# A Nystrom attention and SiLU kernel: the first two batches' attention steps placed anew

## The chip, the cores and the metric

The kernel runs on one core of a Trainium2 chip. The metric is the device time of one execution in microseconds (us); lower is better. A core has five engines that run side by side, each with its own queue of instructions in program order: TensorE (PE, matrix products, whose weight loads the profile lists as PEld), VectorE (DVE), ScalarE (ACT), GpSimd (POOL) and SyncE (SP). POOL and SP issue the DMA transfers here. An instruction waits until what it reads is there and until the buffer that it writes is free; whatever stands behind it in its engine's queue waits with it.

## The reference, cut to what matters

Eight batches of eight heads go through Nystrom attention with 576 tokens, head width 64 and 32 landmarks; the result (4608 tokens of width 512) goes through a two-layer network with SiLU.

```python
q_lm = q.reshape(B, H, m, S // m, D).mean(axis=3)      # m = 32 landmarks of 18 tokens
k_lm = k.reshape(B, H, m, S // m, D).mean(axis=3)
A  = sm(q, k_lm)                                       # softmax of scaled scores
Bm = sm(q_lm, k_lm)
C  = sm(q_lm, k)
Z  = Bm.T / (norm1(Bm) * norm_inf(Bm) + 1e-06)
for _ in range(6):
    Z = 2 * Z - Z @ Bm @ Z
x = A @ Z @ C @ v          # then, over all heads side by side:
h = x @ w_in
out = (h * sigmoid(h)) @ w_out
```

## The kernel before, in words

The attention output x is never formed. For each batch the kernel computes W = C v (`w_mm`, `w_out`), multiplies it by Z (`x_out`, `z_mm`, `z_out`), and then by w_in, which gives a matrix called mb of 256 rows by 2048 columns (`m_unit` makes a quarter of it, `m_pair` two quarters). The first layer of the network is then A times mb (`l1_mm`, products that the profile calls hps), SiLU on ACT (`l1_act`, tile gT), and the second layer is gT times w_out (`l2_mm`, tile ops). These two layers of products fill PE for most of the time.

For each batch b the main loop has 16 steps s. The first eight handle the batch's first tokens (256 of 576 in batch 0, half in the others), the last eight the rest. In step s, `l1_mm(b, s)` makes four hps products, `act` runs SiLU on them, and `l2_mm(n)` issues the next n products of the output tiles that are queued (a tile of 128 tokens takes 16). How many is a table written by hand, `CNT` (lines 764 to 767). Between these, by hand as well, stand the steps of the next batch's attention: the order of instructions on each engine is exactly that of the program.

Batch 0 has nothing to hide behind. Its attention runs ahead of the loop, in lines 772 to 858. There q and k of the first four heads come in float32 over SP (line 122, tiles raw), the rest over POOL's queue (line 105), which casts on the way; DVE casts k (line 774), ACT casts q (line 775). `landmarks_pe` sums the 18 tokens of each landmark on PE (tile lmp), `landmarks_out` scales the sums on ACT (line 212), `transpose_qk` turns q and k on DVE (line 195), `lm_t` turns the landmarks on DVE (line 263), and `bd_expand` copies them into block diagonals (line 271). `b_scores` and `c_scores` are the scores of Bm and C; `b_norm`, `b_scale` and `f_out` prepare the Newton iteration, of which `ns_mm` is the products and `ns_step` the update. `c_exp` is exp(C), `c_transpose` and `c_out` turn it. A is made by `a_scores`, `a_max`, `a_shift`, `a_exp`, then a row sum, a reciprocal and a product on POOL (`a_sum`, `a_rec`, `a_mul`, together `a_norm`), and `a_transpose` and `a_out` bring it to the layout of the first layer (tile AT). Calls of `idle` issue products of zeros on PE, which keep it busy while it would wait.

Batch 1's attention runs inside batch 0's steps. There d is 2, so step s = d + r has r from 1 to 13; the steps from d + 1 on (lines 925 to 1050) carry it. Rest pieces of batch 0 run there too: w_in units 2 and 3 (lines 994 and 1003) and the second part of A (`a0.a_norm(1)`, `a0.a_norm(2)`, `a0.a_transpose(1)`), which `l1_mm(0, 8)` is the first to read.

PSUM buffers are few: pool psa has one (scores sa, products mp, atp, wp, zt), pool pso two (sa, mp, ctp, output tiles ops), pool psn one (lmp, bb). w_in comes in four parts and w_out in four (lines 140 and 145), all over POOL's queue, as do v (line 111) and the later q and k.

Of the kernel before, what the change touches and what calls it, by code (L numbers as in the profile page):

```python
# [40 lines left out]
def kernel(  # L41
# [56 lines left out]
    def load_qk(b, js=(1, 0, 3, 2)):  # L98
        if b not in nat_t:
            nat_t[b] = loadp.tile([128, 4, SEG * Dh], BF, tag="nat", name="nat")  # L100
        nat = nat_t[b]
        for j in js:
            src = (q, k)[j % 2]
            g = j // 2
            nc.gpsimd.dma_start(
                out=nat[:, j, :],
                in_=src[b, 4 * g:4 * g + 4].rearrange("h (l t) d -> (h l) (t d)", t=SEG))
# [21 lines left out]
    def idle(o, n, w=128):  # L129
        for _ in range(n):  # L130
            mm(o[:, 0:w], zero[:, 0:128], zero[:, 0:w], start=True, stop=True)
# [7 lines left out]
    def load_w_in(f):  # L139
        nc.gpsimd.dma_start(  # L140
            out=w_in_sb[:, :, 512 * f:512 * f + 512],
            in_=moe_w_in.rearrange("(j p) n -> p j n", p=128)[:, :, 512 * f:512 * f + 512])

    def load_w_out(j):
        nc.gpsimd.dma_start(
            out=w_out_sb[:, 4 * j:4 * j + 4, :],
            in_=moe_w_out[512 * j:512 * j + 512, :].rearrange("(c p) m -> p c m", p=128))

    load_w_in(0)
    load_qk(1, (1, 0))  # L150
    load_w_in(1)
    load_qk(1, (3, 2))
    load_w_in(2)
# [17 lines left out]

    xb = constp.tile([128, 2, 2 * L], BF, tag="xb", name="xb")
    nc.vector.memset(xb, 0.0)
    parity = constp.tile([128, 2], FP, tag="parity", name="parity")

    eC_t = []
# [59 lines left out]
    class Att:  # L236
# [76 lines left out]
        def b_norm(self):  # L313
            brec = attp.tile([128, 2], FP, tag="brec", name="brec")
            nc.vector.reciprocal(out=brec, in_=self.bsum)
            self.bm = attp.tile([128, 2, L], BF, tag="bm", name="bm")
            nc.vector.tensor_tensor(out=self.bm, in0=self.pb,
                                    in1=brec.unsqueeze(2).to_broadcast((128, 2, L)), op=OP.mult)
            self.bmt = attp.tile([128, 2, L], BF, tag="bmt", name="bmt")
            nc.vector.transpose(out=self.bmt, in_=self.bm)  # L320
            if not self.tiled:
                self.bdt = attp.tile([128, 2, 128], BF, tag="bdt", name="bdt", bufs=1)
                self.expand(self.bdt, self.bmt)
# [14 lines left out]

        def b_scale(self):
            cs = attp.tile([128, 2], FP, tag="cs", name="cs")  # L340
            nc.vector.tensor_reduce(out=cs, in_=self.bmt, op=OP.add, axis=AX.X)
            n1 = attp.tile([128, 2], FP, tag="n1", name="n1")
            nc.vector.tensor_reduce(out=n1, in_=cs.unsqueeze(2).to_broadcast((128, 2, L)),
                                    op=OP.max, axis=AX.X, apply_transpose=True)
            self.nrm = attp.tile([128, 2], FP, tag="nrm", name="nrm")
            w = self.fw = L if self.tiled else 128
            self.fx = nsp.tile([128, 2, w + L], BF, tag=f"fx{w}", name="fx", bufs=3)
            if self.tiled:
                nc.vector.tensor_scalar(out=n1, in0=n1, scalar1=1e-6, scalar2=-1.0, op0=OP.add,
                                        op1=OP.mult)  # L350
                nc.vector.reciprocal(out=self.nrm, in_=n1)
                nc.vector.tensor_tensor(
                    out=self.fx[:, :, w:w + L], in0=self.bm,
                    in1=self.nrm.unsqueeze(2).to_broadcast((128, 2, L)), op=OP.mult)
                return
            nc.vector.tensor_scalar(out=n1, in0=n1, scalar1=1e-6, scalar2=None, op0=OP.add)
            nc.vector.reciprocal(out=self.nrm, in_=n1)
            for g in range(2):
                nc.vector.tensor_scalar(out=self.fx[:, g, w:w + L], in0=self.bm[:, g, :],
                                        scalar1=self.nrm[:, g:g + 1], scalar2=None, op0=OP.mult)  # L360
# [254 lines left out]
        def a_sum(self, i):  # L615
            x, r = self.a_part(i)
            nc.vector.tensor_reduce(out=r, in_=x, op=OP.add, axis=AX.X)  # L617

        def a_rec(self, i, n=1):
            c, _, pr = self.a_dims(i)  # L620
            r = self.arec[0:pr, c:min(c + 2 * n, len(TCH)), :].rearrange("p c h -> p (c h)")
            nc.vector.reciprocal(out=r, in_=r)  # L622
# [118 lines left out]
    def l2_mm(n):  # L741

        st = l2_state
        while n > 0 and st["queue"]:
# [16 lines left out]
                nc.sync.dma_start(out=out[r0:r0 + 128, :], in_=ost)  # L761


    CNT = {0: [0, 0, 0, 0, 6, 4, 2, 2, 4, 2, 2, 2, 2, 2, 2, 2],
           1: [2, 2, 2, 2, 2, 6, 8, 8] + [4, 3] * 4,
           2: [5, 4, 12, 14, 3, 3, 3, 2, 4, 3, 3, 3, 4, 3, 3, 3]}
    REST = [5, 4, 12, 12, 3, 3, 2, 2, 4, 4, 4, 3, 4, 3, 4, 3]
# [1 line left out]

    ORD = (1, 0, 3, 2)  # L770
    wt = pso1("idle")
    idle(wt, 12, 512)
    lp = psn1("lmp")
    nc.vector.tensor_copy(out=nat_t[0][:, 1, :], in_=raw[1])
    nc.scalar.copy(out=nat_t[0][:, 0, :], in_=raw[0])  # L775
    transpose_qk(0, 1)
    landmarks_pe(0, lp, 0, 2)
    transpose_qk(0, 0)
    landmarks_out(0, lp, 0, 2)
    idle(wt, 2, 512)  # L780
    a = Att(0)
    a.lm_t(0)
    a.bd_expand(0, 1, nc.scalar.copy)
    landmarks_pe(0, lp, 3, 1)
    transpose_qk(0, 3)
    landmarks_out(0, lp, 3, 1)
    idle(wt, 2, 512)
    landmarks_pe(0, lp, 2, 1)
    transpose_qk(0, 2)
    landmarks_out(0, lp, 2, 1)  # L790
    idle(wt, 3, 512)
    a.lm_t(1)
    a.b_scores()
    a.bd_expand(1, 1, nc.gpsimd.tensor_copy)
    load_w_in(3)
    a.c_scores()
    a.b_max()
    a.b_exp()
    a.a_start()
    a.a_scores(0)  # L800
    idle(wt, 2, 512)
    a.c_max(0)
    a.c_exp(0)
    a.b_norm()
    a.f_mm()
    a.b_scale()
    a.f_out()
# [2 lines left out]
    a.c_out(0, nc.scalar.copy)  # L810
    a.ns_mm()
    a.c_max(1)
    idle(wt, 2, 512)
    a.ns_step()
    a.c_exp(1)
    a.ns_mm(whole=True)
# [1 line left out]
    a.ns_step(nc.scalar.copy)  # L818
    idle(wt, 1, 512)
    a.c_transpose(1)  # L820
    a.a_shift(0)
    a.a_exp(0)
    a.ns_mm()
    a.c_out(1, nc.scalar.copy)
    a.ns_step()
    a.a_sum(0)
    idle(wt, 1, 512)
    a.ns_mm()
    idle(wt, 2, 512)
    a.ns_step()  # L830
    a.w_scale()
    a.a_rec(0)
    a.a_mul(0)
    load_w_out(0)
    load_w_out(1)
    a.w_mm()
    a.ns_mm()
    a.w_out()
    table(AF.Silu)
    a.ns_step()  # L840
    idle(wt, 1, 512)
    a.ns_mm(last=True)
    a.x_out()
# [4 lines left out]
    a.z_mm(at[:, 1, :])  # L848
    a.z_out()
    lp = psn1("lmp")  # L850
    landmarks_pe(1, lp, 0, 2, (0, 6))

    def first_tokens():
        a.a_transpose(0, at[:, 0, :].bitcast(BF))
        a.a_out(nc.vector.tensor_copy)
        landmarks_pe(1, lp, 0, 2, (6, SEG))

    a.m_unit(0, nc.vector.tensor_copy, nc.scalar.copy, parts=2, between=first_tokens)

# [3 lines left out]
    for b in range(B):  # L863
# [14 lines left out]
        for s in range(NDC):  # L878
# [89 lines left out]
            elif s == d + 2:  # L968
# [20 lines left out]
                a.a_shift(2)  # L989
                a.a_exp(2)  # L990
                if b == 0:
                    a.b_scale()
                    l2_mm(4)
                    a0.m_unit(2, nc.vector.tensor_copy, nc.scalar.copy)
                    a.f_mm()
                    a.f_out()
                    l2_mm(n - 4)
                else:
                    l2_mm(n - 4 - min(n - 4, 6))
                table(AF.Silu)  # L1000
                l1(s)
                if b == 0:
                    a0.m_unit(3, nc.vector.tensor_copy, nc.vector.tensor_copy)
            elif b == 0:
                l1(s)
                r = s - d
                if r == 3:
                    act(s - 1)
                    a.ns_mm()
                    a.c_transpose(0)  # L1010
                    a.ns_step()
                    a.c_out(0, nc.scalar.copy)
                    a0.a_norm(1)
                    a0.a_norm(2)
                elif r == 4:
                    a.ns_mm()
                    a.c_transpose(1)
                    a.w_scale()
                    a.ns_step()
                    a.ns_mm()  # L1020
                    a.c_out(1)
                    a.a_norm(0)
                    a0.a_transpose(1)
                    a0.a_out(nc.scalar.copy)
                elif r == 5:
                    a.ns_step()
                    a.ns_mm()
                    a.a_norm(1)
                elif r == 6:
                    a.w_mm()  # L1030
                    a.ns_step()
                    a.ns_mm()
                    a.w_out()
                    a.ns_step()
                    a.a_norm(2)
                elif r == 7:
                    a.ns_mm(last=True)
                    a.x_out()
                    a.a_transpose(0)
                    a.a_out(nc.scalar.copy)  # L1040
                elif r == 8:
                    a.z_mm(psa1("zt"))
                    a.z_out()
                    l2_mm(cnt[s])
                    a.a_transpose(1)
                    a.a_out(nc.vector.tensor_copy)
                act(s)
                if r in (9, 11):
                    a.m_pair(r - 9)
                l2_mm(cnt[s] if r != 8 else 0)  # L1050
            elif s == d + 3:
                l1(s)
                act(s - 1)
# [114 lines left out]
```

## Time and profile before

| | us |
|---|---|
| median of 3 runs | 267.85 |
| the runs | 266.73, 267.85, 269.39 |
| the profiled execution, its own time | 265.98 |
| its span, first to last instruction | 264.0 |
| PE busy in the span | 254.0 |
| ACT, DVE, POOL busy | 174.3, 161.5, 117.0 |
| start of the first hps product of batch 0 | 23.05 |
| start of the hps products of steps 8 and 11 of batch 0 | 42.07, 47.70 |

The profile is one execution. Its times run from the start of the span. Rows of the timeline name the engine, the line in the kernel, the tile written and the tiles read, and in square brackets how long the engine was idle before and what released it. The chain of work that ended last is followed back from the last instruction, at each step to what released it. A line can be a helper's: line 77 is that of all products.

### The profile page before, as it was taken

How to read it: one execution, taken by the hardware profiler on the slowest of the kernel's cores; microseconds unless marked ns; L12 is line 12 of the kernel's file. 1: busy time of each engine (PE TensorE's matmuls, PEld its weight loads, DVE VectorE, ACT ScalarE, POOL GpSimd, SP SyncE). 2: the span in 40 equal slices, each digit the busy share in tenths (PEclk: the TensorE clock that was granted, in tenths of full speed). 3: DMA queues.
4: the chain of work that ended last, by engine and by line, in shares of the span. 5: the costliest groups of instructions: out<-in, count | busy, mean ns of one | idle time of the engine just before them, and what ended most of it. 6: DMA issues, size and time to landing. Idle time of an engine off the chain costs nothing.

```text
span 264.0 us, 6743 instructions
## 1 busy us (share of the span) xinstructions
PE 254.0 (96%) x2757; PEld 143.1 (54%) x2757; DVE 161.5 (61%) x396; ACT 174.3 (66%) x318; POOL 117.0 (44%) x167
## 2 busy tenths in 40 slices
PE   6798989999999999999999999999999999999994
PEld 2546645475555456455646565555555564555541
DVE  5777975558597868876786778686778653000000
ACT  2457965869747785769575966687577947536511
POOL 8407425214698169744885189408950030100000
PEclk9999999999999999999999999999999999999999
DMA  7999999974996962878197927413371622121122
GB/s 221 204 210 206 201 207 216 195 145 68 184 172 78 201 139 46 148 141 183 50 134 155 196 82 100 118 32 112 50 167 40 103 60 67 40 79 42 40 79 79
DMA packets 37790, 32.93 MB, mean 125 GB/s; under 512 B 18816, under 2 KB 29056, under 8 KB 37760
## 3 DMA queue, kind: packets, MB, share of 16 engines
q0 software_dynamic: 14816, 17.76, 41.8%
q1 hardware_dynamic: 22944, 14.75, 23.2%
q8 instruction: 21, 0.34, 0.5%
q14 instruction: 9, 0.07, 0.1%
HBM read 36.70 MB, written 9.44 MB: 175 GB/s over the span
## 4 chain that ended last, share of the span: by engine, by line
PE 86%; DVE 7%; ACT 2%; DMA 2%; issue 1%; POOL 0%; SPq 0%; ACTq 0%; POOLq 0%; DVEq 0%
PE ops L77 46%; PE hps L77 23%; PE bb L77 3%; PE sa L77 3%; PE lmp L77 3%; PE mp L77 2%; DVE cmx L437 2%; DMA raw<-in_q_dram 2%; DVE nm L580 2%; PE wp L77 2%; PE scp L77 1%; PE mpp L77 1%; PE atp L654 1%; DVE mb L679 1%; DVE xs L593 1%
## 5 line engine op out<-in xcount | busy, mean ns | idle before, releaser
L77 PE MATMUL ops<-w_out_sb,gT 128*128 128x512 bf16 x576 | 146.2, 380 | 0.1
L733 ACT ACTIVATE gT<-hps 128x576 bf16<-128x576 f32 (+2 forms) x128 | 82.4, 650 | 55.3 <-PE hps L77 54.6
L77 PE MATMUL hps<-AT,mb 128*128 128x288 bf16 (+2 forms) x512 | 82.9, 286 | 0.3 <-ACT eC L447 0.2
L77 PEld LDWEIGHTS <-gT 128*128 128x128 bf16 x576 | 52.9, 98 | 47.5 <-issue 5.7
L77 PEld LDWEIGHTS <-mb 128*128 128x128 bf16 x512 | 47.7, 97 | 25.0 <-issue 1.5
L195 DVE STREAM_TRANSPOSE qkT<-nat 128x576 f32<-128x576 f32 x32 | 38.8, 1240 | 0.7 <-ACT nat L775 0.5
L632 POOL TENSOR_TENSOR an<-ex,arec 128x512 bf16<-128x512 bf16 (+2 forms) x24 | 21.1, 902 | 22.9 <-DVE arec L622 20.3
L759 ACT COPY ost<-ops 128x512 f32<-128x512 f32 x36 | 21.0, 582 | 12.1 <-PE ops L77 12.0
L396 DVE SCALAR_TENSOR_TENSOR fx<-fx,bb 128x320 bf16<-128x320 bf16 (+1 forms) x39 | 16.6, 426 | 16.3 <-PE bb L77 15.7
L221 POOL TENSOR_TENSOR lma<-nat 128x1152 f32<-128x1152 bf16 x10 | 23.7, 2372 | 0.0
L699 DVE CAST mb<-mp 128x512 bf16<-128x512 f32 x28 | 18.0, 685 | 9.1 <-PE mp L77 9.1
L1061 POOL CAST gate<-fx 128x2 f32<-128x2 bf16 x6 | 1.1, 185 | 45.4 <-DVE fx L366 45.4
L161 ACT ACT_TABLE_LOAD x16 | 20.5, 1283 | 1.1 <-PEq L1152 0.8
L580 DVE TENSOR_REDUCE nm<-sa 128x16 bf16<-128x512 f32 (+2 forms) x22 | 13.2, 614 | 9.6 <-PE sa L77 9.5
L271 POOL COPY bd<-lmc 32x128 bf16<-32x128 bf16 (+1 forms) x32 | 8.9, 279 | 16.7 <-DVE lmc L263 10.7
L77 PEld LDWEIGHTS <-fx 32*32 32x32 bf16 (+1 forms) x168 | 8.1, 93 | 12.3 <-DVE fx L396 3.4
L700 ACT CAST mb<-mpp 128x1024 bf16<-128x1024 f32 x14 | 14.2, 1011 | 0.6 <-PE mpp L77 0.6
L617 DVE TENSOR_REDUCE arec<-ex 128x16 f32<-128x512 bf16 (+2 forms) x24 | 14.1, 586 | 0.1
L77 PEld LDWEIGHTS <-qkT 128*128 128x128 bf16 (+1 forms) x160 | 10.0, 98 | 6.4 <-DVE xs L593 2.7
L77 PE MATMUL bb<-fx 32*32 32x64 bf16 (+2 forms) x168 | 13.1, 205 | 0.4
L77 PE MATMUL sa<-bd,qkT 128*128 128x128 bf16 (+1 forms) x152 | 12.3, 220 | 0.2 <-DVE xs L593 0.2
L437 DVE TENSOR_REDUCE cmx<-scp 128x1 f32<-128x576 f32 x16 | 11.9, 753 | 0.8 <-PE scp L77 0.5
(112 smaller groups left out, 257.7 us busy)
## 6 DMA issues: line engine op xcount, KB each, us to landing
out_dram<-ost SPq DMA_DIRECT2D x36, 256.0 KB, 2.2
v<-in_v_dram POOLq DMA_DIRECT2D x8, 576.0 KB, 7.6
nat<-in_k_dram POOLq DMA_DIRECT2D x15, 288.0 KB, 6.4
nat<-in_q_dram POOLq DMA_DIRECT2D x15, 288.0 KB, 8.0
w_in_sb<-in_moe_w_in_dram POOLq DMA_DIRECT2D x4, 512.0 KB, 14.9
w_out_sb<-in_moe_w_out_dram POOLq DMA_DIRECT2D x4, 512.0 KB, 12.8
raw<-in_k_dram SPq DMA_DIRECT2D x1, 576.0 KB, 4.1
raw<-in_q_dram SPq DMA_DIRECT2D x1, 576.0 KB, 5.0
```

The costliest lines, as they stand in the source:

```text
L77: nc.tensor.matmul(out=o, lhsT=lhsT, rhs=rhs, start=start, stop=stop, skip_group_check=True)
L161: nc.scalar.activation(out=spare[:, 1:2], in_=spare[:, 0:1], func=func)
L195: nc.vector.transpose(out=o.rearrange("p (l t) -> p t l", t=SEG), in_=nat_t[b][:, j, :].bitcast(FP).rearrange("p (t l) -> p t l", l=L))
L221: nc.gpsimd.tensor_tensor(out=a1, in0=nat[:, :, 0:3 * w], in1=nat[:, :, 3 * w:6 * w], op=OP.add)
L396: nc.vector.scalar_tensor_tensor(out=n, in0=self.fx, scalar=2.0, in1=self.p, op0=OP.mult, op1=OP.add if self.tiled else OP.subtract)
L437: nc.vector.tensor_reduce(out=mx, in_=self.s[g][:, :, 0:HF], op=OP.max, axis=AX.XY, negate=True)
L580: eng.tensor_reduce(out=self.nm[0:pr, c:c + n, :], in_=self.sa[i][0:pr, 0:256 * n].rearrange("p (c h l) -> p c h l", h=8, l=L), op=OP.max, ...
L632: nc.gpsimd.tensor_tensor(out=self.an[0:pr, c:c + n, :].rearrange("p c (h l) -> p (c h) l", l=L), in0=x, in1=r.unsqueeze(2).to_broadcast(( ...
L699: nc.vector.tensor_copy(out=o[:, r, 0:512], in_=m[r])
L700: nc.scalar.copy(out=o[:, :, 512:1024], in_=m2)
L733: nc.scalar.activation(out=gT_t[b][:, 2 * s:2 * s + 2, o + c0:o + c1], in_=h[:, :, 0:c1 - c0], func=AF.Silu)
L759: nc.scalar.copy(out=ost, in_=st["ps"])
```

## The change

Seven edits, all in the first two batches' attention:

- ACT casts the first half of q's columns, POOL the second half; POOL's instruction stands in its queue between two loads of batch 1 and the load of w_in's second part.
- For batch 0, one `lm_t` over both groups of heads follows all landmark sums, and one `bd_expand` on POOL replaces one on ACT and one on POOL.
- For batches 0 and 1, the small constant of the norm is carried in two extra columns of a tile, bme, and the sign is taken in the reduction, in place of a DVE operation of its own.
- In batch 0, `a_scores(0)` comes after `b_norm`, `a_shift` and `a_exp` later in the Newton iteration, and A's sum, reciprocal and product are done in two chunks of 128 tokens by a new function, `a_chunk`, later than before. The issues of w_out's first two parts follow them.
- Most of the idle products' counts in batch 0's attention change, and the landmark sums of batch 1 are split 3 and 15 instead of 6 and 12.
- In batch 1, `c_transpose(0)` and `c_out(0)` move from step d + 3 to step d + 2, `c_out(0)` from ACT to DVE, `b_scale` behind batch 0's w_in unit 2, unit 3 from step d + 2 to step d + 3 with one of its copies on ACT, and the Newton steps, `w_scale`, `a_norm` and batch 0's second part of A are spread otherwise.
- Two of `l2_mm`'s counts for batch 0 change (6 to 4 in step 4, 2 to 4 in step 9), and the four products of step 4 all follow `f_out`.

```diff
     load_qk(1, (1, 0))
+    nc.gpsimd.tensor_copy(out=nat_t[0][:, 0, 9 * Dh:], in_=raw[0][:, 9 * Dh:])
     load_w_in(1)
...
+    bme = constp.tile([128, 2, L + 2], BF, tag="bme", name="bme")
+    nc.vector.memset(bme[:, :, L:L + 1], 9.98377799987793e-07)
+    nc.vector.memset(bme[:, :, L + 1:L + 2], 1.622200012206986e-09)
...
-            nc.vector.tensor_reduce(out=cs, in_=self.bmt, op=OP.add, axis=AX.X)
+            nc.vector.tensor_reduce(out=cs, in_=bme if self.tiled else self.bmt, op=OP.add,
+                                    axis=AX.X)
...
-                                    op=OP.max, axis=AX.X, apply_transpose=True)
+                                    op=OP.max, axis=AX.X, apply_transpose=True,
+                                    negate=self.tiled)
...
-                nc.vector.tensor_scalar(out=n1, in0=n1, scalar1=1e-6, scalar2=-1.0, op0=OP.add,
-                                        op1=OP.mult)
...
+        def a_chunk(self, c):
+            x = self.ex[:, c, :].rearrange("p (h l) -> p h l", l=L)
+            r = self.arec[:, c, :]
+            nc.vector.tensor_reduce(out=r, in_=x, op=OP.add, axis=AX.X)
+            nc.vector.reciprocal(out=r, in_=r)
+            nc.gpsimd.tensor_tensor(
+                out=self.an[:, c, :].rearrange("p (h l) -> p h l", l=L), in0=x,
+                in1=r.unsqueeze(2).to_broadcast((128, 8, L)), op=OP.mult)
...
-    CNT = {0: [0, 0, 0, 0, 6, 4, 2, 2, 4, 2, 2, 2, 2, 2, 2, 2],
+    CNT = {0: [0, 0, 0, 0, 4, 4, 2, 2, 4, 4, 2, 2, 2, 2, 2, 2],
...
-    idle(wt, 12, 512)
+    idle(wt, 14, 512)
...
-    nc.scalar.copy(out=nat_t[0][:, 0, :], in_=raw[0])
+    nc.scalar.copy(out=nat_t[0][:, 0, 0:9 * Dh], in_=raw[0][:, 0:9 * Dh])
...
-    idle(wt, 2, 512)
-    a = Att(0)
-    a.lm_t(0)
-    a.bd_expand(0, 1, nc.scalar.copy)
+    idle(wt, 1, 512)
     landmarks_pe(0, lp, 3, 1)
...
-    idle(wt, 3, 512)
-    a.lm_t(1)
+    idle(wt, 5, 512)
+    a = Att(0)
+    a.lm_t(0, 2)
     a.b_scores()
-    a.bd_expand(1, 1, nc.gpsimd.tensor_copy)
+    a.bd_expand(0, 2, nc.gpsimd.tensor_copy)
...
     a.a_start()
-    a.a_scores(0)
-    idle(wt, 2, 512)
     a.c_max(0)
     a.c_exp(0)
     a.b_norm()
+    a.a_scores(0)
+    idle(wt, 1, 512)
     a.f_mm()
...
     a.c_transpose(1)
+    a.ns_mm()
+    a.c_out(1, nc.scalar.copy)
     a.a_shift(0)
+    a.ns_step()
     a.a_exp(0)
     a.ns_mm()
-    a.c_out(1, nc.scalar.copy)
+    idle(wt, 1, 512)
+    a.w_scale()
     a.ns_step()
-    a.a_sum(0)
-    idle(wt, 1, 512)
-    a.ns_mm()
-    idle(wt, 2, 512)
-    a.ns_step()
-    a.w_scale()
-    a.a_rec(0)
-    a.a_mul(0)
-    load_w_out(0)
-    load_w_out(1)
     a.w_mm()
     a.ns_mm()
+    a.a_chunk(0)
     a.w_out()
     table(AF.Silu)
     a.ns_step()
+    a.a_chunk(1)
+    load_w_out(0)
+    load_w_out(1)
...
-    landmarks_pe(1, lp, 0, 2, (0, 6))
+    landmarks_pe(1, lp, 0, 2, (0, 3))
...
                 if b == 0:
-                    a.b_scale()
-                    l2_mm(4)
+                    a.c_transpose(0)
+                    a.c_out(0)
                     a0.m_unit(2, nc.vector.tensor_copy, nc.scalar.copy)
                     a.f_mm()
+                    a.b_scale()
                     a.f_out()
-                    l2_mm(n - 4)
+                    l2_mm(n)
...
                 if b == 0:
-                    a0.m_unit(3, nc.vector.tensor_copy, nc.vector.tensor_copy)
+                    a.ns_mm()
...
                 if r == 3:
+                    a.ns_step()
                     act(s - 1)
-                    a.ns_mm()
-                    a.c_transpose(0)
-                    a.ns_step()
-                    a.c_out(0, nc.scalar.copy)
+                    a0.m_unit(3, nc.vector.tensor_copy, nc.scalar.copy)
                     a0.a_norm(1)
-                    a0.a_norm(2)
                 elif r == 4:
                     a.ns_mm()
                     a.c_transpose(1)
+                    a.ns_step()
+                    a.c_out(1)
+                    a0.a_norm(2)
+                elif r == 5:
+                    a.ns_mm()
+                    a.ns_step()
                     a.w_scale()
-                    a.ns_step()
-                    a.ns_mm()
-                    a.c_out(1)
-                    a.a_norm(0)
                     a0.a_transpose(1)
                     a0.a_out(nc.scalar.copy)
-                elif r == 5:
+                    a.a_norm(0)
+                elif r == 6:
+                    a.w_mm()
+                    a.ns_mm()
                     a.ns_step()
+                    a.w_out()
+                    l2_mm(2)
                     a.ns_mm()
                     a.a_norm(1)
-                elif r == 6:
-                    a.w_mm()
                     a.ns_step()
-                    a.ns_mm()
-                    a.w_out()
-                    a.ns_step()
-                    a.a_norm(2)
                 elif r == 7:
                     a.ns_mm(last=True)
                     a.x_out()
+                    a.a_norm(2)
                     a.a_transpose(0)
...
-                l2_mm(cnt[s] if r != 8 else 0)
+                l2_mm(cnt[s] - {8: cnt[s], 6: 2}.get(r, 0))
```

More of the change, by code (lines that the diff above doesn't have):

```diff
@@ L318, in b_norm @@
                                     in1=brec.unsqueeze(2).to_broadcast((128, 2, L)), op=OP.mult)
-            self.bmt = attp.tile([128, 2, L], BF, tag="bmt", name="bmt")
+            if self.tiled:
+                self.bmt = bme[:, :, 0:L]
+            else:
+                self.bmt = attp.tile([128, 2, L], BF, tag="bmt", name="bmt")
             nc.vector.transpose(out=self.bmt, in_=self.bm)
@@ L812 @@
     a.c_max(1)
-    idle(wt, 2, 512)
+    idle(wt, 1, 512)
     a.ns_step()
@@ L820 @@
     a.c_transpose(1)
+    a.ns_mm()
+    a.c_out(1, nc.scalar.copy)
     a.a_shift(0)
+    a.ns_step()
     a.a_exp(0)
     a.ns_mm()
-    a.c_out(1, nc.scalar.copy)
+    idle(wt, 1, 512)
+    a.w_scale()
     a.ns_step()
-    a.a_sum(0)
-    idle(wt, 1, 512)
-    a.ns_mm()
-    idle(wt, 2, 512)
-    a.ns_step()
-    a.w_scale()
-    a.a_rec(0)
-    a.a_mul(0)
-    load_w_out(0)
-    load_w_out(1)
     a.w_mm()
     a.ns_mm()
+    a.a_chunk(0)
     a.w_out()
@@ L855, in first_tokens @@
         a.a_out(nc.vector.tensor_copy)
-        landmarks_pe(1, lp, 0, 2, (6, SEG))
+        landmarks_pe(1, lp, 0, 2, (3, SEG))
     a.m_unit(0, nc.vector.tensor_copy, nc.scalar.copy, parts=2, between=first_tokens)
```

## The prediction

> **What bounds the kernel now.** I read the cores view first (one core, granted clock 1.000, span 264.0 us), then the page's busy shares, the table of windows, the chain that ended last in two windows, and the timelines of the engines from 0 to 72 us. The page says that TensorE (PE) is the bound on the whole, and the rows from 48 us on agree: in the chain of 27 to 58 us nothing but PE stands behind 46 us. So time saved ahead of that point is carried to the end one for one, and only there can this change act.
>
> ```profile
> PE 254.0 (96%) x2757; PEld 143.1 (54%) x2757; DVE 161.5 (61%) x396; ACT 174.3 (66%) x318; POOL 117.0 (44%) x167
> ```
>
> Ahead of it PE's busy share misleads, because matmuls on zeros ("idle") fill its waits. The chain (start, length, what) shows what is really waited for up to the first products of batch 0:
>
> ```profile
> 1.27 4.99 DMA raw<-in_q_dram
> ...
> 6.28 1.16 ACT nat L775
> ...
> 7.48 1.18 PE lmp L77 x18
> ...
> 8.68 0.35 ACT lmn L212 x2
> ...
> 9.05 0.26 DVE lmc L263
> ...
> 9.33 0.25 ACT bd L271
> ...
> 10.36 0.23 ACT lmn L212
> ...
> 10.63 0.69 PE lmp L77 x18
> 11.32 0.65 PE idle L77 x3
> ...
> 14.67 0.18 DVE n L349
> ...
> 21.34 0.49 PE lmp L77 x6
> ```
>
> Read here: q's landing, its cast, landmarks, four copies on ACT that stand before another landmark copy, and so on: one operation's latency after another. The second stretch is batch 1's attention, threaded between products of batch 0:
>
> ```profile
> 33.82 0.69 DVE mb L679
> ...
> 36.18 0.68 DVE mb L679
> ...
> 39.13 0.61 POOL an L632
> ...
> 40.38 0.69 ACT AT L661
> 41.07 0.51 ACT gT L733
> ...
> 41.62 0.61 PE ops L77 x2
> ```
>
> PE waits there for copies of w_in units, then for POOL's product, PE's transpose and ACT's copy of A. Below, l1(s) is the group of four hps products of step s; l1(8) starts at 42.07 and l1(11) at 47.70 in PE's timeline.
>
> DMA is the third view. w_out's rows give 10.5, 12.8 and 17.7 us to landing; the last issue, at 23.77, is the 17.7, so w_out's last quarter lands near 41.4. The products that need it (12 to 15 of the first output tile) start at 41.62: before, they just miss a wait.
>
> **Part 1, the halved cast.** ACT's cast of 1152 columns takes 1.15 us; gT's 576 columns take 0.65, so half ends at 6.93 instead of 7.43. POOL's half has no row of its own kind. POOL's plain copies: 1.04 us for 1024 columns (L737), 1.27/4 = 0.32 for 128 (L271), a slope of 0.80 ns, which gives 0.68 us for 576. Two-input sums of float32 (L224, 1.00 us for 384) would give 1.5, and a multiply's 902 ns for 512 about 1.0; the copy of 128 columns, 0.32, is the floor. I take 0.68, a copy being nearest, ending at 6.98. The landmark products then start at 7.0, not 7.48. Their last nine need POOL's half only at 7.5; the DVE transpose of q needs it at 7.0 with about 0.25 us to spare, so the cast costs nothing until 0.95 us and one for one after. POOL also waits for q's landing (6.26) with w_in(1) behind it: issued 5.80 before, about 7.0 now; the next k load moves from 6.54 to 7.75. DMA moved 207 to 216 GB/s from 0 to 30 us with earlier loads still queued, and the q load behind waited until 7.92 anyway; I take nothing (bounds 0 and +1.2 us on the landings).
>
> The page GPSIMD Engine Reference of the Trainium skill (Key points) says that POOL shares its SBUF interfaces with DVE and is hindered by DVE instructions in a two-port mode. If DVE's transpose held POOL until 6.99, the cast would end at 7.7 and the prologue's gain would shrink by 0.45 us. The trace disagrees for transposes: POOL's sum L221 takes 2.36 us at 67.94 beside reductions and 2.37 at 77.11 beside transposes.
>
> **Part 2, one landmark transpose.** lm_t(0) (0.24) and four ACT copies (1.00) leave the middle; one DVE transpose of 128 columns (0.31 by batch 2's row) follows the last landmarks, and POOL's four copies grow from 1.04 to 1.27 us (batch 1's row). The k landmarks start when the first landmark copies end (8.55), the last q landmarks when ACT has read those (9.56, was 10.63): 1.07 us earlier, of which 0.5 is part 1. DVE's four transposes run back to back (7.05 + 3 x 1.16 = 10.55), the landmark transpose ends near 10.9. But five idle matmuls at 0.216 now follow the landmarks on PE: 9.56 + 0.53 + 1.08 = 11.17, and b_scores starts at 11.2, was 11.90: 0.70 earlier. POOL's copies end at 12.2, under c_scores (1.18 us), so a_scores is not held; w_in(3) goes out at 12.2, was 12.91.
>
> **Part 3, the norm's constants.** One 0.17 us DVE operation with its gap goes, 0.20 us, in both batches; the two extra memsets lie in DVE's 1.48 us wait for k. f_out: 0.90 earlier.
>
> **Part 4, batch 0's order.** From c_max(1) to the fourth Newton step the row waits go: the third Newton product no longer stands behind a_shift (0.3 us), and a_sum's 0.69 no longer precedes step 4. Step 4 runs at 17.6, was 19.04. Then costs come back: eCT's second copy ends at 17.5, so w_mm (0.49) starts at 17.6 and the fifth product at 18.1; a_chunk(0) (reduction of 256 columns 0.38, reciprocal 0.20) stands before step 5, a_chunk(1) before x_out, some 0.1 and 0.2 us late. x_out: 19.35, was 20.51. POOL multiplies 256 columns twice at about 0.6 (64x256 took 0.61), the second done at 20.05; the transpose of A needs it near 20.7. The two w_out issues moved behind it go out at 20.05 instead of 20.72. With three landmark matmuls instead of six in front, w_in's unit 0 starts 1.35 earlier, but the rest must still be done: PE is back to back until the first hps at 21.9, was 23.05. **Prologue: -1.15 us** (bounds -0.5 and -1.7, by the cast and by the two chunk delays).
>
> **Part 5, batch 1.** All starts 1.15 earlier. Up to a_exp nothing is changed. Then:
> - c_transpose(0) comes first and runs in PE's shadow; DVE's copy (0.55, ACT's was 0.80) fits before w_in's unit 2, which waits for the exp of a_scores(1) (ACT, ends 33.30 before, 32.15 now). PE had four ops products before that unit and now has them after f_mm: 0.65 us idle.
> - b_scale now stands behind unit 2's DVE copy (0.69): f_out ends at 34.4 (34.63 before). l1(4) ends at 34.1, so the first Newton product waits 0.4 us, ahead of l1(5).
> - Unit 3's second copy is on ACT (0.58) beside DVE's (0.69): the 0.70 idle before c_transpose goes.
> - a0's second normalization stands behind c_out(1): DVE 37.55 to 38.6, POOL to 39.25, PE's transposes to 39.85, ACT's copy to 40.6. PE has only two ops products beside it: idle 0.7 and 0.35. l1(8) starts at 40.6, was 42.07; it now has two ops products and one Newton product (0.6 us) still owed.
> - Products 12 to 15 come at 41.8, 0.4 us behind w_out's landing; v's landing (22.99 + 16.1 = 39.1) is ahead of w_mm at 41.15.
> - a_norm(1) of batch 1 waits on DVE behind Newton step 4: reduction and reciprocal end at 43.2, POOL's 1.03 at 44.3, and the transpose of A's first part, on PE at 43.65, waits 0.6 us. Before, that product was done at 43.03, ahead of use at 45.02.
>
> l1(11) then starts near 47.2, was 47.70, with the same 22 ops products done on both sides. So the region gives back 0.6 of the 1.15 (bounds: nothing, if POOL is early; 2.2, if each of those waits grows by half). SP issues nothing anew.
>
> **Sum.** The profiled execution took 265.98 us, 1.98 around its span of 264.0: 265.98 - 1.15 + 0.60 = 265.4. It stands 1.87 below the median of the three runs (267.85); on that footing 267.3.
>
> **The rivals.**
> - *Nothing is given back.* Units and copies mesh, and POOL's multiplies are done before PE asks: -1.2 to -1.5, about 266.5. For it: ACT is relieved of 0.80 + 1.00 us. Against: w_out's landing at 41.4 stops products 12 to 15 from coming earlier than 41.45, and a_norm(1) is plainly queued behind a step.
> - *Slower.* The copy of A's second part (DVE, POOL, PE, ACT, some 2.9 us from c_out(1) to ACT's end) stands one step nearer its reader l1(8). If it ends 0.55 us later than I have it, the gain is gone; at 42.0 the result is +0.85, 268.7. For it: POOL an and ACT AT are on the chain already. Against: ACT and DVE each have a gap before it.
> - *The clock.* PE's first zero products start 0.427 us apart, and 0.216 from 4.86 us on. If the thinner filling let the clock fall back once, for a stretch as long as that rise (3.6 us), PE's part of the chain there, 1.87 us by the two lmp rows above (1.18 and 0.69), would double: +1.3 in all, 269.2. The granted clock stayed 1.000 through a PE gap of 1.69 us, and the change shortens that gap. The page TensorE: Matmul & The Clock Gate of the Trainium skill (Part 1) sets the fall at an idle window of about 3.4 us; by it nothing happens here, and the trace agrees as far as 1.69 us goes.
>
> **How the numbers follow.** Forecast 0.50 (its own range 266.6 to 268.0), nothing given back 0.25, slower 0.20, clock 0.05. The predicted time is the forecast's, 267.3. The range runs from the second case with the prologue's upper bound (267.85 - 1.7 - 0.4 for the runs' scatter) to the slower ones: 265.6 to 268.9. A measurement of this kernel tells about 1% (2.7 us) from no change, the three runs being 1.0% apart. No case reaches that alone: faster 0.11 (second case with a low draw), same 0.80, slower 0.09 (the two slow cases with a high draw).
>
> **What would show it.** Landmarks (lmp) start at 7.0; bb<-lmc at 11.2; x at 19.35; the first hps at 21.9; l1(8) at 40.6; PE idle before atp near 43.7 with POOL an as its releaser; l1(11) at 47.2. I am wrong if POOL's cast takes over 0.95 us, if a wait for w_out shows at 41 to 42 us, if the first hps comes after 22.5, or if the last part from 48 us on is not the 216 us that it is now.

## The result and the profile after

The changed kernel took 265.81 us (median of 22 runs, 265.47 to 271.0), the kernel before 267.41 (22 runs, 266.33 to 270.94): a ratio of 0.9952, 95% interval 0.9934 to 0.9970. The ratio compares the fast runs of both kernels, without the one slow run that each had; by it the change is worth 1.3 us (0.8 to 1.8), and the two medians are 1.6 us apart. That is under 1%, which the prediction had as "same" (0.80). The time is inside the predicted range, but only 0.2 us above its lower end and 1.5 us below the predicted 267.3. The profiled execution of the changed kernel took 265.63 us with a span of 263.86, against 265.98 and 264.0 before: only 0.35 us less. So the profiles show about a quarter of what the runs show, and this is what the experiments had to settle.

The page's busy shares of the changed kernel. PE is still the bound, with the same work:

```profile
PE 254.5 (96%) x2755; PEld 143.4 (54%) x2755; DVE 161.1 (61%) x397; ACT 173.1 (66%) x314; POOL 118.3 (45%) x169
```

The chain that ended last in the changed kernel (start, length, what), from the first landmarks to the copies of A in batch 1:

```profile
7.03 1.18 PE lmp L77 x18
...
8.62 0.70 PE lmp L77 x18
...
9.62 0.69 PE lmp L77 x18
10.30 1.08 PE idle L77 x5
11.38 0.20 PE bb L77 x16
...
22.05 0.44 PE hps L77 x4
...
38.87 0.62 POOL an L650
...
39.53 0.56 PE atp L672 x4
40.12 0.70 ACT AT L679
40.86 0.70 PE hps L77 x4
...
43.60 1.04 POOL an L650
...
44.69 0.40 PE atp L672 x4
```

The first landmarks start 0.45 us earlier than before, the last q landmarks 1.01 earlier (9.62 for 10.63), and the row of idle products that now follows them takes a part of it back. The first hps of batch 0 starts at 21.88 in PE's timeline, where it was 23.05: the work ahead of the loop is 1.17 us shorter. Then batch 1 gives it back. POOL's product `an`, PE's transpose of it and ACT's copy stand in front of l1(8) at 40.86 (42.07 before, still 1.21 ahead), and the next `an` in front of the transpose at 44.69. l1(11) starts at 47.68, where it was 47.70. PE's timeline of the kernel before, and of the changed kernel:

```profile
47.70 0.72 PE L77 MATMUL hps<-AT,mb 128*128 128x320 bf16 x4
```

```profile
47.68 0.72 PE L77 MATMUL hps<-AT,mb 128*128 128x320 bf16 x4
```

From there to the end both spans are 216 us. Of the 0.35 us between the two profiled executions 0.14 lie in the span and 0.21 around it; of the 0.14 only some 0.01 lie ahead of l1(11), so in the profiles the region that the change touches gains next to nothing.

POOL's timeline of the changed kernel gives the price of the one operation that had no row before (start, busy, engine, line, form, and the idle time ahead with its releaser):

```profile
6.34 0.66 POOL L151 CAST nat<-raw 128x576 bf16<-128x576 f32 x1 [0.52 <-DMA raw<-in_q_dram]
```

The forecast had 0.68 us for it.

### The profile page after: what moved, and what is told of

Same layout as the page of the kernel before. It is cut to its first block, busy times and chain, and to the rows that moved or that the text cites. A ratio compares the mean times of both kernels' runs of the same rounds, so it can differ in the third digit from the quotient of the medians.

```text
span 263.9 us, 6736 instructions
## 1 busy us (share of the span) xinstructions
PE 254.5 (96%) x2755; PEld 143.4 (54%) x2755; DVE 161.1 (61%) x397; ACT 173.1 (66%) x314; POOL 118.3 (45%) x169
## 4 chain that ended last, share of the span: by engine, by line
PE 85%; DVE 7%; ACT 4%; DMA 2%; issue 1%; POOL 1%; ACTq 0%; POOLq 0%
PE ops L77 46%; PE hps L77 23%; PE lmp L77 3%; PE bb L77 3%; PE sa L77 3%; PE mp L77 2%; DVE cmx L445 2%; DMA raw<-in_k_dram 2%; PE scp L77 1%; PE wp L77 1%; PE mpp L77 1%; ACT eC L455 1%; ACT ex L614 1%; DVE nm L588 1%; PE atp L672 1%
## 5 line engine op out<-in xcount | busy, mean ns | idle before, releaser
L650 POOL TENSOR_TENSOR an<-ex,arec 128x512 bf16<-128x512 bf16 (+2 forms) x23 | 20.1, 897 | 18.0 <-DVE arec L640 16.0
L276 POOL COPY bd<-lmc 32x128 bf16<-32x128 bf16 x32 | 9.2, 286 | 15.0 <-DVE lmc L268 9.0
L625 DVE TENSOR_REDUCE arec<-ex 128x16 f32<-128x512 bf16 (+2 forms) x23 | 13.4, 584 | 0.0
```

The costliest lines, as they stand in the source:

```text
L650: nc.gpsimd.tensor_tensor(out=self.an[0:pr, c:c + n, :].rearrange("p c (h l) -> p (c h) l", l=L), in0=x, in1=r.unsqueeze(2).to_broadcast(( ...
```

## The experiments

Twelve kernels ran, each beside runs of the kernel before on the same chip. The theories, for the 1.0 us that the two profiles don't show: A, the clock's rise at the start; B, the landing of w_out's last quarter, which a usual run of the kernel before waits for; C, the early start, which would carry the whole gain alone; and, after the first eight runs, D, that w_mm of batch 2 waits for the DMA transposes of exp(C), which run beside POOL's loads, with E as its rival, that the difference lies elsewhere. In some executions of most of these kernels the mean granted clock is 0.994 or below. e9's profiled execution is one of them and shows what happens: the clock falls to half for 3.41 us, which by itself takes the mean over a span of 264 us to 0.994 (its own is 0.991, as the clock is at half again in its last 1.5 us). The column "full clock" in the table below is the median of the runs whose mean clock was at least 0.997, so that this doesn't blur differences of half a microsecond.

**1. Is it the clock in the first microseconds?** The change raised the opening filler from 12 to 14 idle products.

```diff
-    idle(wt, 12, 512)
+    idle(wt, 14, 512)
```

This alone in the kernel before:

> The kernel before with 14 idle products instead of 12 in front, nothing else. Theory A (the runs' medians differ by more than the two profiles because the PE clock rises later, or falls back once, in many executions of the kernel before, its idle products ending 1.7 us ahead of the landmark products): median 0.8 to 1.5 us under the kernel before, and its runs scatter less. Rival B (the medians differ because w_out's last quarter lands just about when the kernel before needs it, and later in other executions): no change, within 0.3 us.

And undone in the changed kernel:

> The changed kernel with 12 idle products instead of 14 in front. Theory A: 0.8 to 1.5 us slower than the changed kernel, so about the kernel before. Rival B: as the changed kernel, about 1.3 us under the kernel before.

Measured 267.08 (ratio 0.9998, 0.9978 to 1.0018) and 265.94 (0.9971, 0.9949 to 0.9994). The two products are worth nothing either way, so theory A falls. But e1's profiled execution was a usual one, with a span of 264.9 where the profile of before has 264.0, and its PE timeline shows two waits that the profile of before doesn't have. Before:

```profile
41.62 0.61 PE L77 MATMUL ops<-w_out_sb,gT 128*128 128x512 bf16 x2
...
72.81 0.65 PE L77 MATMUL wp<-v,eCT 96*32 96x64 bf16 x48
```

e1:

```profile
42.15 0.38 PE L77 MATMUL ops<-w_out_sb,gT 128*128 128x512 bf16 x1 [0.56 <-DMA w_out_sb<-in_moe_w_out_dram]
...
74.01 0.36 PE L77 MATMUL wp<-v,eCT 96*32 96x64 bf16 x24 [0.31 <-DMA eCT<-eC]
```

The first is the wait for w_out's last quarter that the prediction had as "they just miss a wait". The second is in batch 2, where the change touches nothing: w_mm waits for the DMA that transposes exp(C). The first wait, 0.56 us, and what batch 2's stretch took more than in the profile of before, 0.40, are about the 0.88 us by which the two spans differ.

**2. The halves.** The changed lines ahead of the loop with the old loop and counts, and the reverse:

> The changed kernel ahead of the loop, the old order of batch 1 inside it (and the old counts). If what the profile shows is all (first hps 1.17 us earlier, and w_out's landing at 41.5 holding the products 12 to 15 that would come at 40.5): l1(11) 0 to 0.4 us earlier than before, l1(8) about 42. Theory A gives this kernel the whole gain in the median, 0.8 to 1.5 us. Rival B gives no gain: it waits for w_out in every execution, and in step 7 rather than in step 8.

> The old order ahead of the loop, the changed order of batch 1 inside it. By the profiles the loop's new order costs 0.6 to 1.2 us against the old one when nothing comes earlier: l1(11) at 48.3 to 48.9. Theory A: 0.6 to 1.2 us slower than the kernel before, with its scatter. Rival B: the products that need w_out's last quarter come 1.2 us later, so the scatter goes, and the median is the same to 0.5 us slower.

Measured 266.34 (0.9975, 0.9960 to 0.9990) and 268.06 (1.0039, 1.0017 to 1.0061). The kernel with the early start alone is 0.7 us faster, the one with the new order of the loop alone 1.0 slower; together they gain 1.3. They are not additive, and theory C, the early start alone, falls short. e3's PE timeline says why the early start alone gains so little: it runs into w_out's landings.

```profile
33.43 0.59 PE L77 MATMUL ops<-w_out_sb,gT 128*128 128x512 bf16 x2 [0.94 <-DMA w_out_sb<-in_moe_w_out_dram]
...
41.49 0.38 PE L77 MATMUL ops<-w_out_sb,gT 128*128 128x512 bf16 x1 [0.72 <-DMA w_out_sb<-in_moe_w_out_dram]
```

In the changed kernel these products stand later in the order (products 12 to 15 at 42.15, landing at 41.55), and PE does work of batch 1 in that time. So the new order costs little on the early start, where what it delays would have waited anyway (l1(11) at 47.68 for e3's 47.55), and its full price on the old one (e4's 49.08 for 47.70, later than the 48.3 to 48.9 that I expected). Part of the two times is not the order's own, though. e3's l1(11) is only 0.15 us ahead of that in the profile of before; but e3's w_mm of batch 2 doesn't wait for the transposes (batch 2's stretch takes 13.22 us, for 13.57 in e1), and e4's waits 0.31 us for them (13.76). And e3's profiled execution, 265.82, is the shortest of its twelve runs.

**3. Is it w_out's landing alone?** Two ways to take that wait from the kernel before: its products later, or its load one place earlier in POOL's queue.

```diff
-    CNT = {0: [0, 0, 0, 0, 6, 4, 2, 2, 4, 2, 2, 2, 2, 2, 2, 2],
+    CNT = {0: [0, 0, 0, 0, 4, 4, 2, 2, 4, 4, 2, 2, 2, 2, 2, 2],
```

> The kernel before with the changed kernel's counts alone (four products instead of six in step 4, four instead of two in step 9), so that products 12 to 15 of the first output tile come one step later, 42.7 instead of 41.6. Theory B (the kernel before mostly waits for w_out's last quarter there, by an amount that varies with its landing at 41.4 to 42.1): median 0.3 to 0.8 us under the kernel before. Rival C (the median gain comes from the earlier start alone, the wait being hidden elsewhere): within 0.2 us of the kernel before.

```diff
     load_w_out(2)
-    load_v(1)
     load_w_out(3)
+    load_v(1)
```

> The kernel before with the issues of w_out's last quarter and of batch 1's v exchanged, so that w_out's last quarter lands near 39 and v near 41.4, ahead of w_mm at 42.7. Theory B: the wait at 41.6 goes in every execution: median 0.5 to 1.0 us under the kernel before, and l1(8) at 42.1 or a little earlier. Rival C: within 0.2 us of the kernel before.

Measured 266.98 (1.0008, 0.9985 to 1.0032) and 267.01 (1.0005, 0.9984 to 1.0025). In neither profile does PE wait for w_out at 41 to 42 us, and by the ratio neither is faster. The profiles show time lost in batch 2 instead: w_mm waits for the transposes there, 0.25 and 0.29 us in e5, 0.21 and 0.31 in e6. That landing varies: e6 issues the first transpose at 63.85, as the profile of before does (63.83), and it lands at 73.06 for 72.44. Theory B, w_out alone, isn't borne out, nor is it excluded for e5: the interval of e6 leaves out the 0.5 to 1.0 us expected of it, that of e5 reaches 0.4 us, and at full clock the runs of e5 are 0.8 us and those of e6 0.3 us below the runs of before beside them (266.50 and 266.96 for 267.27).

**4. The waits that remain in batch 1.** The two normalizations of A placed earlier in the changed kernel, so that POOL's `an` is done when PE asks; and the same with v loaded behind w_out's last quarter and w_mm two products later.

```diff
                     a.c_out(0)
+                    a0.a_sum(2)
...
                     a.f_out()
+                    a0.a_rec(2)
+                    a0.a_mul(2)
...
-                    a0.a_norm(2)
...
                     a.a_norm(0)
+                    a.a_norm(1)
...
-                    a.a_norm(1)
```

> The changed kernel with batch 1's a_norm(1) one step earlier, and the sum of A's last 64 tokens of batch 0 right after c_out(0), its reciprocal and product after f_out. If the loop gives back the prologue's gain through the two waits for POOL (0.70 us before atp at 39.5, 0.32 us at 44.7): both go, l1(8) at 40.1 to 40.4, l1(11) at 46.9 to 47.3, and the median is 0.4 to 0.8 us under the changed kernel. If what holds the loop is w_out's landing: products 12 to 15 wait at 41.5, and at most 0.3 us is gained.

> As the one before, and in addition v of batch 1 is loaded after w_out's last quarter, and w_mm with w_out() comes after the two products 12 and 13. If w_out's landing holds the one before, this gains 0.2 to 0.5 us more; if not, the same within 0.2 us, or 0.3 slower where w_mm waits for v at 41.4.

Measured 265.52 (0.9950, 0.9932 to 0.9968) and 265.42 (0.9938, 0.9917 to 0.9960). Both waits for POOL are gone, l1(8) starts at 40.12 in e7 and l1(11) at 46.92, 0.76 us earlier than in the changed kernel. So l1(8) and l1(11) came where they were expected, but e7's median is only 0.3 us under the changed kernel, for 0.4 to 0.8 expected. At full clock the medians are 265.22 and 264.91, against 265.67: e7 keeps some 0.45 us of its 0.76, and e8, with l1(11) at 46.93, all of it. What e7 loses, its profile shows behind l1(11), in batch 2, whose stretch takes 13.44 us (13.16 in e8, 13.07 in the changed kernel): w_mm comes earlier there and waits for a transpose, though POOL makes no stop between its loads. PE's timeline of e7:

```profile
72.59 0.36 PE L77 MATMUL wp<-v,eCT 96*32 96x64 bf16 x24 [0.20 <-DMA eCT<-eC]
```

Ahead of l1(11), in place of POOL, PE now waits for w_out in e7, and for v in e8, where v is last. In e7:

```profile
41.89 0.38 PE L77 MATMUL ops<-w_out_sb,gT 128*128 128x512 bf16 x1 [0.41 <-DMA w_out_sb<-in_moe_w_out_dram]
```

and in e8:

```profile
41.94 0.56 PE L77 MATMUL wp<-v,eCT 96*32 96x64 bf16 x48 [0.41 <-DMA v<-in_v_dram]
```

The same 0.41 us, with the two loads exchanged: what PE waits for there is the end of POOL's row of loads, whichever is last. Over all runs neither kernel can be told from the changed one, or from the other, by its interval.

**5. Why batch 2's transposes are late.** POOL issues four loads of q and k at 62 to 64 us, beside SP's two transposes. POOL's timeline of the kernel before has a stop between the first and the second:

```profile
62.80 0.53 POOL L105 DMA_DIRECT2D nat<-in_q_dram  x1 [0.23 <-issue]
```

All five kernels so far with the old lines ahead of the loop (before, e1, e4, e5, e6) show that stop (0.22 to 0.24 us), none of those with the new lines does. From issue to landing the first transpose took 8.96 to 9.25 us in e1, e4, e5 and e6, 8.61 in the profile of before, and 8.24 to 8.82 in the five with the new lines. POOL's timeline of the changed kernel:

```profile
62.53 0.55 POOL L105 DMA_DIRECT2D nat<-in_q_dram  x1
```

The change puts two more instructions into POOL's queue (169 for 167). Two memsets put into POOL's idle time in the kernel before, at the start:

```diff
+    for _ in range(2):
+        nc.gpsimd.memset(gate, 0.0)
```

> The kernel before with two tiny memsets more on POOL, in its idle time ahead of batch 0's scores; they only shift the place of every later POOL instruction in its queue by two. Theory D (the median gain is a wait in batch 2, 25 us behind the change: PE's w_mm waits for the DMA transposes of exp(C), which run beside four q and k loads; in the kernels with the old order ahead of the loop POOL stops 0.23 us between these loads, in those with the new order not, which has two POOL instructions more there): the 0.23 us stop goes, wp waits less, median 0.3 to 0.8 us under the kernel before. Rival E (the stop and the wait have nothing to do with POOL's count of instructions): stop, wait and median as in the kernel before, within 0.2 us.

And two of the four loads moved away from the transposes, to the end of batch 1:

```diff
-                    load_qk(b + 3)
+                    load_qk(b + 3, (1, 0) if b == 1 else (1, 0, 3, 2))
...
                     ready.bd_expand(0, 2, nc.gpsimd.tensor_copy)
+                    load_qk(4, (3, 2))
```

> The kernel before with two of the four loads of batch 4's q and k issued at the end of batch 1 instead of beside the DMA transposes of batch 2's exp(C). Theory D: the transposes land 1 us or more before w_mm, no wait at wp, the interval between batch 1's SiLU number 24 and number 32 falls to 13.1 us, the median 0.5 to 0.9 us under the kernel before. If the transposes' place in the median is small: within 0.2 us.

The same edit in the changed kernel, and in e8:

> The changed kernel with the same two loads later. Theory D: it waits there in few executions, so the median falls by at most 0.3 us, and the runs near 267.2 mostly go. The difference to the kernel before with later loads is then what the change itself is worth: 0.2 to 0.7 us.

> The norms earlier, v last, and the two loads later, in one kernel: the parts of the earlier runs together. Interval between batch 1's SiLU number 24 and number 32 13.1 us in every execution; median 264.5 to 265.2, 0.5 to 1.2 us under the changed kernel.

e10 settles that the wait in batch 2 is part of a usual run of the kernel before: 266.38 (0.9975, 0.9960 to 0.9990), 0.6 us less at full clock, with nothing changed but the place of two loads. SP's timeline of the kernel before, start and length of the issue of the two transposes:

```profile
63.83 5.05 SPq L454 DMA_TRANSPOSE eCT<-eC  x2
```

and of e10:

```profile
64.03 2.76 SPq L454 DMA_TRANSPOSE eCT<-eC  x2
```

They land at 69.56 and 70.20 us, for 72.44 and 73.05 in the profile of before. PE's timeline of e10 has its w_mm of batch 2 whole and without a wait, and the wait for w_out still there:

```profile
41.84 0.38 PE L77 MATMUL ops<-w_out_sb,gT 128*128 128x512 bf16 x1 [0.33 <-DMA w_out_sb<-in_moe_w_out_dram]
...
73.00 0.56 PE L77 MATMUL wp<-v,eCT 96*32 96x64 bf16 x48
```

e9 removed POOL's stop as expected,

```profile
63.85 0.55 POOL L105 DMA_DIRECT2D nat<-in_q_dram  x1
```

and its w_mm had no wait; but its gain, 0.4 us at full clock, has an interval that reaches 1 (0.9990, 0.9977 to 1.0003). That the stop is what tips the transposes is not shown: e10 still has it (0.24 us) and doesn't wait, e7 hasn't and does.

e11 took 266.66 (0.9983, 0.9960 to 1.0005). It gains nothing at full clock over the changed kernel, as it must if that kernel has no such wait. Half of its runs had the fall of the clock and took 267.35 to 267.87, where I had expected the runs near 267.2 to go. What the change is worth where neither kernel waits for the transposes is the step from e10 to e11, 0.47 us at full clock, within the 0.2 to 0.7 expected; over all runs e11 is 0.28 us slower than e10. e12 took 265.49 (0.9944, 0.9925 to 0.9963) and missed what I expected: with all together it is no better than e8, and v has become the wait, as PE's timeline of e12 shows:

```profile
42.28 0.55 PE L77 MATMUL wp<-v,eCT 96*32 96x64 bf16 x48 [0.81 <-DMA v<-in_v_dram]
```

All runs together (batch 2's stretch: from the end of SiLU no. 24 to that of no. 32 in the profiled execution, code that the change leaves alone):

| kernel | median us | ratio, 95% interval | full clock us | batch 2's stretch us |
|---|---|---|---|---|
| before | 267.41 | 1 | 266.91 to 267.27 | 13.17 |
| changed | 265.81 | 0.9952, 0.9934 to 0.9970 | 265.67 | 13.07 |
| e1, before with 14 | 267.08 | 0.9998, 0.9978 to 1.0018 | 267.08 | 13.57 |
| e2, changed with 12 | 265.94 | 0.9971, 0.9949 to 0.9994 | 265.86 | 13.08 |
| e3, early start alone | 266.34 | 0.9975, 0.9960 to 0.9990 | 266.27 | 13.22 |
| e4, loop alone | 268.06 | 1.0039, 1.0017 to 1.0061 | 267.95 | 13.76 |
| e5, products later | 266.98 | 1.0008, 0.9985 to 1.0032 | 266.50 | 13.85 |
| e6, w_out earlier | 267.01 | 1.0005, 0.9984 to 1.0025 | 266.96 | 13.83 |
| e7, norms early | 265.52 | 0.9950, 0.9932 to 0.9968 | 265.22 | 13.44 |
| e8, and v last | 265.42 | 0.9938, 0.9917 to 0.9960 | 264.91 | 13.16 |
| e9, two on POOL | 266.65 | 0.9990, 0.9977 to 1.0003 | 266.53 | 13.08 |
| e10, late load | 266.38 | 0.9975, 0.9960 to 0.9990 | 266.31 | 13.07 |
| e11, changed, late load | 266.66 | 0.9983, 0.9960 to 1.0005 | 265.84 | 13.08 |
| e12, e8, late load | 265.49 | 0.9944, 0.9925 to 0.9963 | 265.04 | 13.07 |

The ratios are to the runs of before beside each kernel, whose full-clock medians were 267.06 (e1 to e4), 267.27 (e5 to e8) and 266.91 (e9 to e12); a few tenths between kernels of different groups say little.

## Why the prediction was right, and where it was not

**The early start: right.** Landmarks at 7.03 (7.0 forecast), bb at 11.31 (11.2), x at 19.44 (19.35), first hps at 21.88 (21.9): 1.17 us for the forecast's 1.15. POOL's cast is a plain copy by its price. The loads that it pushed back landed within 0.2 us of where they did: w_in(1) at 20.12 (20.31 before), w_out's last quarter at 41.55 (41.42), so taking nothing for them was right.

**The waits of batch 1: the right places, sizes too small.** f_out ended at 34.35 (34.4 forecast). PE's wait for POOL's `an` ahead of the first transpose is 0.70 (0.7), its wait for ACT's copy ahead of l1(8) 0.24 (0.35), and the later transpose of A waits 0.32 (0.6) with POOL as its releaser. But POOL ended the first product at 39.48 and not at 39.25, and l1(8) came 0.26 late for that; from l1(8) to l1(11) another 0.22 came to it. l1(11) is at 47.68, 47.2 forecast: the region gave back 1.15 us, not 0.60. That is the mis-sized term of the sum. e7 shows that the waits for POOL were real: with the two norms earlier they vanish and l1(11) comes 0.76 us earlier.

**The step that failed: "on that footing 267.3".** The forecast for the profiled execution, 265.4, is 0.2 from the 265.63 that it took. I then added the 1.87 us by which the profile of before stood below the median, as if both kernels' profiles stood so. They do not. Before's profiled execution, 265.98, is shorter than all but 2 of the 126 timed runs of that kernel; the changed kernel's, 265.63, is a usual run of it (265.67 at full clock). What a usual run of before has on top of its profile are, as far as the runs show, the two DMA waits: e10 takes away the one for the transposes, 0.6 us at full clock, and the one for w_out, which e10 still has, took 0.33 us there and 0.56 in e1. 265.98 + 0.6 + 0.33 to 0.56 makes 266.9 to 267.1, and 266.9 to 267.3 were measured. The changed kernel has neither wait in its profile: its products 12 to 15 come 0.6 us after w_out's landing, and its transposes land 0.7 and 0.3 us ahead of the products of w_mm that read them (72.06 and 72.69 for 72.79 and 72.98). So 0.35 us of its gain is the difference of the two profiles, and some 1.0 is put down to the waits of the usual run that it escapes. Of these the transposes' 0.6 is shown, by e10. The price of w_out's wait in the median is argued from the profiles of e1 and e10, and the 0.47 us from e10 to e11 fit it: no run takes both waits from the kernel before, and e5 and e6, which take w_out's alone, don't show it by their ratios.

That the time is inside the range is luck in part. The lower end was taken from the case "nothing is given back", which didn't happen, with the prologue's upper bound, which wasn't reached; and 267.85 - 1.7 - 0.4 is 265.75, where the range says 265.6.

**The rivals.** "Nothing is given back" named nearly the measured change (-1.2 to -1.5) with the wrong reason: batch 1 did give back all. "Slower" needed l1(8) at 42.0; it came at 40.86. The clock rival, which I gave 0.05, does happen, in both kernels (in 11 of 35, 4 of 35 and 6 of 34 runs of before, in 5 of 22 of the changed one): in the changed kernel, the runs whose mean clock was 0.994 took 267.28, 1.6 us more than the others. My reason against it was that a gap of 1.69 us of PE had left the clock up. That reason falls. The table of windows (stretch, us, busy us and count of PE, PEld, DVE, ACT and POOL, granted clock, DMA share, GB/s) for an execution of e9 where it fell:

```profile
18.10:21.50 3.40, 2.25 (x88) 1.67 (x89) 2.02 (x9) 2.71 (x6) 1.97 (x3) 0.98 1.16 211
21.50:24.90 3.40, 3.40 (x38) 2.29 (x36) 2.46 (x5) 0.72 (x3) 2.86 (x4) 0.51 1.22 206
```

and the same stretches of the kernel before, where it did not:

```profile
18.10:21.50 3.40, 2.53 (x87) 1.50 (x87) 2.22 (x9) 2.73 (x5) 1.78 (x2) 1.00 1.16 213
21.50:24.90 3.40, 3.37 (x50) 2.33 (x48) 2.66 (x5) 2.13 (x9) 3.05 (x5) 1.00 1.21 205
```

The fall came after a stretch in which PE was busy for 2.25 of 3.4 us and no gap was longer than 0.5, so it is not the longest gap that counts. Nor is it the busy share of one such stretch alone: in e7 PE was busy for 2.01 of 3.41 us, with no gap above 0.43, and the clock stayed:

```profile
17.63:21.04 3.41, 2.01 (x93) 1.63 (x90) 2.13 (x10) 2.52 (x6) 2.02 (x4) 1.00 1.18 211
21.04:24.45 3.41, 3.38 (x45) 2.52 (x43) 3.41 (x7) 2.51 (x8) 2.98 (x4) 1.00 1.20 205
```

The page TensorE: Matmul & The Clock Gate of the Trainium skill (Part 1) asks for an idle window of about 3.4 us. The length agrees with the 3.41 us for which the clock stayed down; that the window has to be idle doesn't agree with the row of e9.

**What stays open.** Why some kernels draw the fall more often than others (6 of 12 runs of e11, none of 12 of e1, 6 of 34 of before beside e11) isn't settled. Whether the two DMA waits of the kernel before add up isn't either, as no run takes both away. What makes POOL stop for 0.23 us between two loads is open too. In the profile of before an 8 KB packet of the instruction queue moves at 63.28 us, close by, and in the changed kernel at 61.72, so a fetch of instructions at a fixed count is the nearest guess. It is not shown, and the packet moves 0.5 us after the end of the stop.

## What to carry to other kernels

Before you add a difference between two profiles to a median, look where each profiled execution stands among the timed runs of its own kernel: one that is shorter than nearly all of them has missed waits that the usual run has. A load that lands just in time in the profile is a cost in part of the runs, and should enter the sum as such; here two such waits account for some 1.0 us by the reckoning above, more than all that the edits did to the profile. Where PE is the bound and a landing stands fixed in the middle, time saved ahead of it is lost there unless the order puts other work in its place (e3's 21.62 for 23.05 at the first hps left 0.15 us at l1(11)), so an early start and a new order have to be tried together and apart.

## What the runs showed of the hardware

- Two DMA transposes of exp(C), issued by SP, took 7.8 to 8.5 us to landing (the median of the two) beside four loads of 288 KB from POOL's queue and 4.8 to 5.2 beside two; SP was held by their issue for 4.2 to 5.6 us and for 2.8.
- POOL stopped for 0.22 to 0.24 us between two loads in the six kernels with one count of instructions ahead of them (before, e1, e4, e5, e6, e10); with two memsets more in POOL's idle start (e9) it is gone from between the two loads.
- The granted clock fell to 0.5 for 3.41 us after a stretch in which PE was busy two thirds of the time with no gap above 0.5 us (e9), and stayed up after one in which PE was busy 2.01 of 3.41 us (e7). In the changed kernel the runs with a mean clock of 0.994 took about 1.6 us more.
